# Attention inside a fused MoE kernel: scores of a step in one tile of two PSUM banks, one exponential of 768 columns, and a bank shared by maxima and small products

## The chip, the cores and the metric

The kernel runs on one core of a Trainium2 chip. The metric is the device time of one execution in microseconds (us). Before the change three runs gave 666.51, 666.72 and 667.41 us, median 666.72 us.

## The reference

Three stages follow each other: an attention whose mask compares hash buckets of queries and keys, a mixture of experts with one expert per token, and a two-layer block with a clipped gate. The change is in the attention alone (2 batches, 8 heads each, 768 positions, 64 dimensions per head).

```python
def _attn_ref(q, k, v, proj):
    scale = 1.0 / np.sqrt(D)
    q_bits = np.einsum('bhsd,dk->bhsk', q, proj) > 0
    k_bits = np.einsum('bhsd,dk->bhsk', k, proj) > 0
    mask = q_bucket[:, :, :, None] == k_bucket[:, :, None, :]
    scores = np.where(mask, scale * np.matmul(q, k.T), -1e9)
    attn = np.exp(scores - np.max(scores, axis=-1, keepdims=True))
    attn = attn / (np.sum(attn, axis=-1, keepdims=True) + 1e-09)
    return np.matmul(attn, v)

x = _attn_ref(q, k, v, proj)        # then tokens x 512
x = _moe_ref(x, w_gate, w1, w2, capacity)
return _moe2_ref(x, w_in, w_out)    # h * clip(h + 3, 0, 6) / 6 between two products
```

## The kernel before

The schedule is written out by hand: each engine runs its instructions in the order in which the program issues them, and an engine waits where an operand or a buffer isn't free. The attention is a loop of 96 steps (16 heads with 6 blocks of 128 keys, `STEPS = NC * NH`, L753 and L826 to L847), with a tail of six more turns. One turn `k` issues, in this order:

1. what is due at `k - 0.5` (helpers that were booked for a time in steps with `at` and `spread`, L771 to L782);
2. on ScalarE `high(k - 1)`: a copy of the exponentials in 16 bits (`phi`);
3. `scores(k)` (L437): for each half of 384 queries two matmuls into one PSUM tile `pst` (L445, L446), and one exponential on ScalarE from there into half of the SBUF tile `pf` (L447);
4. `low(k - 2)`: the rest `plo = pf - phi`, on GpSimd, or on VectorE;
5. `mx(k + 8)` (L422): the row maxima, eight steps ahead: for each half one matmul into a tile `psm` (L428) and one VectorE reduction from it (L431);
6. in odd turns `pv(k - 5)` and `pv(k - 4)` (L463): 18 small matmuls each, which add a head's sums over the values (`psv`);
7. what is due at `k`.

Helpers book further work into the same queues: `bits(g)` (L392) makes the hash bits of four heads, two tiles `psb` that VectorE reads at L390; `vgate(r)` (L528) multiplies values of two heads by the gate's weights, tile `psg`, read by VectorE at L546 and L547 for one head and, a step later, for the other; `vscale(g)` (L564) takes the largest value of four heads through a transpose `psn` and a product `pso`; `route` (L208) and `any_unmatched` (L608) use one tile each. `vsplit(h)` (L678) prepares the values of a head on ScalarE and VectorE (L686). `evac(h)` (L495) divides a finished head's sums on VectorE (L483, L486, L491); it is booked by `Q["ev"]` half a step after the turn that issues the head's last sums (L804).

PSUM has eight banks of 512 columns of 32 bits. They stand in four pools, and a tile of a pool takes the next of its buffers in turn; the first instruction that writes it waits until the last reader of the tile that was there is done:

```python
        ps_t = opened(actx, "ps_t", 2, space=PSUM)
        ps_m = opened(actx, "ps_m", 3, space=PSUM)
        ps_v = opened(actx, "ps_v", 2, space=PSUM)
        ps_x = opened(actx, "ps_x", 1, space=PSUM)
```

So scores have two banks, maxima three, the sums over values two, and all the small products of the helpers (`misc`, L346) one. At the start of the kernel the tiles of `ps_v` also hold the first bits (`psb0`, L727), and `ps_t` and `ps_v` hold idle matmuls (`heat`, L321) that keep TensorE busy.

Of the kernel before, what the change touches and what calls it, by code (L numbers as in the profile page):

```python
# [19 lines left out]
P = 128  # L20
# [43 lines left out]
def moe_attention_kernel(ctx, tc, qk, v, vt, pj, wg, w1, w2, win, wout, out, cap):  # L64
# [142 lines left out]

    def route(b, psum):  # L208

# [26 lines left out]
        yield  # L236
        dve.tensor_tensor(out=sc, in0=k3, in1=o, op=ALU.mult)
        yield
        dve.tensor_reduce(out=pos[:, b], in_=sc, axis=AX.X, op=ALU.add)
# [61 lines left out]

    Q = {'v': (-3.25, -4.75, -1.75, -2.25), 'vg': (-4.5, -4.75), 'vgd': 1, 'pr': (-13.0, -12.75, -12.0, -12.5), 'prd': 0.6, 'b0': 7.75, 'b': 1.75, 'bd': 0.5, 'vm0': (8.0, 8.25, 10.75, 13.0), 'vm': (-0.5, 4.75, 7.0, 12.25), 'vs': 13.25, 'pa': 1.5, 'ev': 0.5, 'lvt': -5.0, 'v4': (2.0, 3.75, 4.0, 16.25), 'vg0': (1.85, -4.4, 7.75), 'p2': 3.5, 'lr': (0, 3, 1.5, 4.5), 'lv': 5.5, 'vsd': 0.75, 'ac': (0, 0, 2, 6, 7, 8, 9, 10), 'hd': (3, 5, 17), 'hn': (1, 3, 2, 0, 2, 0, 0, 0), 'ap': (0,), 'h0': (7,), 'hl': (4, 7, 10), 'l0': (), 'll': (1,), 'ht': (6, 3, 7, 6, 3, 2)}

# [3 lines left out]
    with ExitStack() as actx:  # L307
# [4 lines left out]
        ps_t = opened(actx, "ps_t", 2, space=PSUM)  # L312
        ps_m = opened(actx, "ps_m", 3, space=PSUM)
        ps_v = opened(actx, "ps_v", 2, space=PSUM)
        ps_x = opened(actx, "ps_x", 1, space=PSUM)

        idle_sb = pa.tile([P, 512], F16, tag="idle", name="idle_sb")
# [3 lines left out]
        def heat(pool_, tag, n, cols=512):  # L321

            if pool_ not in heat_t:
                heat_t[pool_] = pool_.tile([P, 512], F32, tag=tag, name=f"heat{tag}")
            for _ in range(n):
                pe.matmul(heat_t[pool_][:, :cols], idle_sb[:, 0:P], idle_sb[:, :cols], start=True, stop=True)
# [17 lines left out]
        vr_t, vt_t, vh_t, am_t, sc_t, sw_t = {}, {}, {}, {}, {}, {}  # L344

        def misc(name):  # L346
            return ps_x.tile([P, 512], F32, tag="x", name=name)

# [43 lines left out]
        def bits(g, tiles=None):  # L392
# [20 lines left out]
            for n in range(2):  # L413
                if not tiles:
                    for i in range(4):
                        dot(n, i)
                    yield
                rows(n)
                if not tiles:
                    yield  # L420

        def mx(n):  # L422
# [3 lines left out]
            for n in range(2):  # L426
                ps = ps_m.tile([P, 512], F32, tag="m", name=f"psm{h}{c}{n}")
                pe.matmul(  # L428
# [8 lines left out]
        def scores(k):  # L437
            h, j = divmod(k, NC)
            st = sets[h % 4]
            pf = pf_t[k] = pt.tile([P, S], F32, tag="pf", name=f"pf{k}", bufs=4)  # L440
            kc = slice(j * P, (j + 1) * P)
            for n in range(2):
                ps = ps_t.tile([P, 512], F32, tag="t", name=f"pst{k}{n}")
                qc = slice(n * HS, (n + 1) * HS)
                pe.matmul(ps[:, :HS], st["K1"][:, kc], st["Y"][:, qc], start=True, stop=False)  # L445
                pe.matmul(ps[:, :HS], st["K2"][0:77, kc], st["X"][0:77, qc], start=False, stop=True)  # L446
                act.activation(  # L447
                    pf.rearrange("k (c n p) -> k c n p", c=NC, n=2)[:, :, n],
                    ps[:, :HS].rearrange("k (p c) -> k c p", c=NC), AF.Exp, scale=0.125 / SC / SC,
                )  # L450

# [11 lines left out]
        def pv(k):  # L463
            h, j = divmod(k, NC)
            if j == 0:
                pv_t[h] = ps_v.tile([P, 512], F32, tag="v", name=f"psv{h}")
            hi, lo = phi_t.pop(k), plo_t.pop(k)
# [60 lines left out]
        def vgate(r):  # L528
# [13 lines left out]
            for hh in range(2):  # L542
# [6 lines left out]
                    op0=ALU.mult, op1=ALU.subtract,  # L549
                )  # L550
                yield

# [11 lines left out]
        def vscale(g, fresh=misc):  # L564
# [14 lines left out]
            am2 = ph.tile([n, 1], F32, tag=f"am2{n}", name=f"am2{g}")  # L579
            dve.tensor_reduce(out=am2, in_=ps[0:n, 0:P], axis=AX.X, op=ALU.max)  # L580
            if n > 1:
                a, am2 = am2, ph.tile([n, n], F32, tag="dg", name="dg")
# [6 lines left out]
            a = ph.tile([P, n], F32, tag=f"am3{n}", name=f"am3{g}")  # L589
            dve.tensor_copy(a, ps[:, 0:n])  # L590
            a = a.bitcast(I32)
            x = ph.tile([P, 2 * n - 1], I32, tag=f"ex{n}", name=f"ex{g}")
# [116 lines left out]
        act.activation(st["K2"][0:D], r0[D:P], AF.Copy, scale=SC)  # L709
        pre = [prep(h, h == 0) for h in range(3)]  # L710
        for n in range(2):
            for i, t in enumerate(("X", "K2")):
                c = slice(n * HS, (n + 1) * HS)
                ps = (ps_m, ps_t)[i].tile([P, 512], F32, tag="mt"[i], name=f"psf{n}{i}")
                pe.matmul(
# [10 lines left out]
        DOT = (5,)  # L726
        b0 = bits(0, [ps_v.tile([P, 512], F32, tag="v", name=f"psb0{n}") for n in range(2)])  # L727
        for n in range(NC):
# [72 lines left out]
        for h in range(NH):  # L801
# [6 lines left out]
            elif h < NH - 1:  # L808
                at(k + Q["pa"], pair, h // 2)
                at(NC * h + Q["lvt"], load_vt, h // 2 + 1)  # L810
        spread(66, route(0, lambda: misc("psr0")), 1.5)
        spread(84, weigh(0))
# [699 lines left out]
```

## Time and profile before

| what | value |
|---|---|
| median of three runs | 666.72 us |
| the profiled execution's own time | 666.91 us |
| its span, first to last instruction | 665.2 us |
| TensorE matmul busy | 635.3 us (96%) |
| VectorE busy | 478.9 us (72%) |
| ScalarE busy | 425.3 us (64%) |
| GpSimd busy | 226.5 us (34%) |
| maxima, L431 on VectorE, x192 | 96.3 us, 548 ns each |
| exponentials, L447 on ScalarE, x192 | 83.4 us, 486 ns each |
| attention, first to last sum over values | 36.2 to 233.9 us |

The times come from one execution that the hardware profiler recorded. A line of the trace has the start, the length, the engine, the source line, the operation and its tiles; in brackets stands how long the engine had been idle before it, and which engine, tile and line ended that. PE is TensorE's matmul, PEld its loading of weights, DVE VectorE, ACT ScalarE, POOL GpSimd. Matmuls overlap, so that the distance from start to start says more than the lengths do.

### The profile page before, as it was taken

The page shows a single profiled execution, that of the slowest core. Times are in us where ns is not written, and L with a number is a line of the kernel's source. Part 1 is how long each engine was busy: PE and PEld are TensorE (multiplying, and loading weights), DVE is VectorE, ACT ScalarE, POOL GpSimd, SP SyncE. Part 2 cuts the span into 40 slices and gives each one's busy share as a digit, 9 for nine tenths or more (in the row PEclk, how much of TensorE's full clock was granted, in tenths as well). Part 3 has the DMA queues.
Part 4 walks back from the last instruction along what each step waited for, and adds up shares of the span by engine and source line. Part 5 has one row for each costly group of instructions (what it writes and reads, how often), then busy time and mean ns, then how long its engine had stood idle before and what let it go on. Part 6 is the DMA issues. An engine that isn't in the chain of part 4 may idle for free.

```text
span 665.2 us, 14405 instructions
## 1 busy us (share of the span) xinstructions
PE 635.3 (96%) x5534; PEld 479.4 (72%) x5534; DVE 478.9 (72%) x1041; ACT 425.3 (64%) x867; POOL 226.5 (34%) x198
## 2 busy tenths in 40 slices
PE   6899999999999879999999999999999999999893
PEld 2689888889898749999999996555555555555541
DVE  6778888898999888888888887888888342222320
ACT  2668878778787747777667765544555586555830
POOL 5357869769778133121366500000000021000011
PEclk8989999999999899999999999999999999999998
DMA  8685764774464339877677733444441010000011
GB/s 240 144 227 136 239 171 125 219 182 119 102 175 154 101 100 316 265 242 241 216 255 252 235 117 99 154 148 138 152 134 64 1 63 33 1 0 1 1 49 52
DMA packets 38642, 94.14 MB, mean 142 GB/s; under 512 B 9146, under 2 KB 14522, under 8 KB 38562
## 3 DMA queue, kind: packets, MB, share of 16 engines
q1 hardware_dynamic: 35474, 85.71, 43.1%
q0 software_dynamic: 2400, 7.36, 3.2%
q8 instruction: 46, 0.75, 0.5%
q14 instruction: 34, 0.28, 0.1%
q10 hardware_dynamic: 688, 0.03, 0.1%
HBM read 67.14 MB, written 6.29 MB: 110 GB/s over the span
## 4 chain that ended last, share of the span: by engine, by line
PE 55%; ACT 3%; DMA 2%; DVE 2%; issue 1%; POOL 0%; POOLq 0%; DVEq 0%
PE psg L1287 16%; PE pso L1314 15%; PE psy L1065 11%; PE psh L1038 11%; DMA out_dram<-os,inv 2%; ACT junk L1241 1%; PE psa L1015 1%; ACT gh L1297 1%; DVE rl L1290 1%; ACT rl L1289 0%; PE heat L1117 0%; DVE wl L164 0%; POOL out_dram L1329 0%; PE psw L296 0%; DVE os L1321 0%
## 5 line engine op out<-in xcount | busy, mean ns | idle before, releaser
L461 POOL TENSOR_TENSOR plo<-pf,phi 128x768 f16<-128x768 f32 x85 | 145.0, 1732 | 45.1 <-ACT phi L455 21.4
L447 ACT ACTIVATE pf<-pst 128x384 f32<-128x384 f32 x192 | 83.4, 486 | 44.5 <-PE pst L446 41.2
L431 DVE TENSOR_REDUCE mx<-psm 128x1 f32<-128x384 f32 x192 | 96.3, 548 | 21.5 <-PE psm L428 21.3
L1329 POOL DMA_INDIRECT out_dram<-os,inv x12 | 12.2, 1014 | 270.6 <-DVE os L1321 244.3
L164 DVE SCALAR_TENSOR_TENSOR wl<-raw,wh 128x1024 f16<-128x1024 f32 (+1 forms) x68 | 83.2, 1227 | 5.9 <-ACT wh L158 5.2
L1287 PE MATMUL psg<-yTh,ch 128*128 128x512 f16 (+1 forms) x256 | 83.4, 326 | 3.2 <-DVE rl L1290 3.2
L1287 PE MATMUL psg<-yTl,ch 128*128 128x512 f16 (+1 forms) x256 | 83.4, 326 | 0.0
L1287 PE MATMUL psg<-yTh,cl 128*128 128x512 f16 (+1 forms) x256 | 83.4, 326 | 0.0
L1290 DVE SCALAR_TENSOR_TENSOR rl<-rl,psg 128x512 f32<-128x512 f32 x64 | 35.0, 550 | 64.5 <-ACT rl L1289 64.0
L445 PE MATMUL pst<-Y,K 128*128 128x384 f32 x192 | 75.4, 393 | 1.8 <-ACT pf L447 1.7
L1287 PEld LDWEIGHTS <-ch 128*128 128x128 f16 x512 | 50.1, 98 | 35.9
L1314 PE MATMUL pso<-ch,gh 128*128 128x512 f16 x192 | 72.8, 379 | 0.0
L1314 PE MATMUL pso<-ch,gl 128*128 128x512 f16 x192 | 72.8, 379 | 0.0
L1314 PE MATMUL pso<-cl,gh 128*128 128x512 f16 x192 | 72.8, 379 | 0.0
L455 ACT ACTIVATE phi<-pf 128x768 f16<-128x768 f32 x83 | 70.0, 844 | 1.9
L428 PE MATMUL psm<-K,X 76*128 76x384 f32 x192 | 65.8, 421 | 4.7 <-DMA X<-b 2.1
L1314 PEld LDWEIGHTS <-gh 128*128 128x128 f16 x384 | 37.6, 98 | 42.3
L158 ACT ACTIVATE wh<-raw 128x1024 f16<-128x1024 f32 (+1 forms) x68 | 67.6, 998 | 0.5 <-issue 0.5
L1065 PE MATMUL psy<-hh,wl 128*128 128x224 f16 x256 | 66.3, 259 | 0.0
L1065 PE MATMUL psy<-hh,wh 128*128 128x224 f16 x256 | 66.3, 259 | 0.0
L1065 PE MATMUL psy<-hl,wh 128*128 128x224 f16 x256 | 66.3, 259 | 0.0
L446 PE MATMUL pst<-X,K 77*128 77x384 f32 x192 | 66.1, 344 | 0.0
(231 smaller groups left out, 1494.6 us busy)
## 6 DMA issues: line engine op xcount, KB each, us to landing
raw<-in_w_dram SPq DMA_DIRECT2D x64, 512.0 KB
rc<-in_win_dram SPq DMA_DIRECT2D x16, 512.0 KB
rc<-in_wout_dram SPq DMA_DIRECT2D x16, 512.0 KB
r<-in_qk_dram SPq DMA_DIRECT2D x16, 384.0 KB
K<-hi SPq DMA_DIRECT2D x31, 192.0 KB
vr<-in_v_dram SPq DMA_DIRECT2D x4, 768.0 KB
vt<-in_vt_dram SPq DMA_DIRECT2D x8, 384.0 KB
Y<-hi SPq DMA_DIRECT2D x16, 192.0 KB
```

The lines of the kernel that those rows point to most:

```text
L158: act.activation(wh[e, i][:, c : c + n], r, AF.Copy, scale=(S1, S2)[i // 2])
L164: dve.scalar_tensor_tensor(out=wl[e, i][:, c : c + n], in0=r, scalar=(S1, S2)[i // 2], in1=wh[e, i][:, c : c + n], op0=ALU.mult, op1=ALU.s ...
L431: dve.tensor_reduce(out=mm[:, c, n : n + 1], in_=ps[:, :HS], axis=AX.X, op=ALU.max)
L445: pe.matmul(ps[:, :HS], st["K1"][:, kc], st["Y"][:, qc], start=True, stop=False)
L446: pe.matmul(ps[:, :HS], st["K2"][0:77, kc], st["X"][0:77, qc], start=False, stop=True)
L447: act.activation(pf.rearrange("k (c n p) -> k c n p", c=NC, n=2)[:, :, n], ps[:, :HS].rearrange("k (p c) -> k c p", c=NC), AF.Exp, scale=0 ...
L455: act.activation(phi_t[k], pf_t[k], AF.Copy)
L461: eng.tensor_tensor(out=plo_t[k], in0=pf_t.pop(k), in1=phi_t[k], op=ALU.subtract)
L1038: pe.matmul(ps, l[:, c], r[:, k], start=n == 0, stop=n == 3 * KD - 1)
L1065: pe.matmul(ps, l, r, start=n == 0, stop=n == 3 * KF - 1)
L1287: pe.matmul(ps, l, x, start=n == 0, stop=n == 3 * KD - 1)
L1314: pe.matmul(po[blk][s], l, r, start=first and n == 0, stop=last and n == 2)
```

## The change

- `ps_t` keeps two buffers, but a buffer is now a tile of two banks (`pair_of`). `scores(k)` writes both halves into one such tile with its four matmuls, and one exponential of 768 columns follows in place of two of 384.
- `ps_m` has two buffers in place of three, and `ps_v` one in place of two. Every third tile of the maxima is taken from `ps_x`, the bank of the small products, unless a small product is in use by the program's order (`in_use`, set by `misc` and cleared by `misc_read` where the last reader has been issued).
- `evac` is booked at the turn itself (`Q["ev"]` is 0.0 in place of 0.5), so that VectorE gets it ahead of what is due half a step later.
- At the start the first bits (`psb`) and the first products for head 0 (`psf`) use the paired tiles.

```diff
-        ps_m = opened(actx, "ps_m", 3, space=PSUM)
-        ps_v = opened(actx, "ps_v", 2, space=PSUM)
+        ps_m = opened(actx, "ps_m", 2, space=PSUM)
+        ps_v = opened(actx, "ps_v", 1, space=PSUM)
         ps_x = opened(actx, "ps_x", 1, space=PSUM)
+
+        def one_of(pool_, tag, name):
+            return pool_.tile([P, 512], F32, tag=tag, name=name)
+
+        def pair_of(name):
+            return ps_t.tile([P, 2, 512], F32, tag="t", name=name)
...
+        in_use = [False]
+        nmx = [0]
+
         def misc(name):
-            return ps_x.tile([P, 512], F32, tag="x", name=name)
+            in_use[0] = True
+            return one_of(ps_x, "x", name)
+
+        def misc_read():
+            in_use[0] = False
+
+        def for_mx(name):
+            nmx[0] += 1
+            if nmx[0] % 3 or in_use[0]:
+                return one_of(ps_m, "m", name)
+            return one_of(ps_x, "x", name)
...
                 rows(n)
                 if not tiles:
+                    misc_read()
                     yield
...
-                ps = ps_m.tile([P, 512], F32, tag="m", name=f"psm{h}{c}{n}")
+                ps = for_mx(f"psm{h}{c}{n}")
...
+            ps = pair_of(f"pst{k}")
             for n in range(2):
-                ps = ps_t.tile([P, 512], F32, tag="t", name=f"pst{k}{n}")
                 qc = slice(n * HS, (n + 1) * HS)
-                pe.matmul(ps[:, :HS], st["K1"][:, kc], st["Y"][:, qc], start=True, stop=False)
-                pe.matmul(ps[:, :HS], st["K2"][0:77, kc], st["X"][0:77, qc], start=False, stop=True)
-                act.activation(
-                    pf.rearrange("k (c n p) -> k c n p", c=NC, n=2)[:, :, n],
-                    ps[:, :HS].rearrange("k (p c) -> k c p", c=NC), AF.Exp, scale=0.125 / SC / SC,
-                )
+                pe.matmul(ps[:, n, :HS], st["K1"][:, kc], st["Y"][:, qc], start=True, stop=False)
+                pe.matmul(ps[:, n, :HS], st["K2"][0:77, kc], st["X"][0:77, qc], start=False, stop=True)
+            act.activation(
+                pf.rearrange("k (c n p) -> k n c p", c=NC, n=2),
+                ps[:, :, :HS].rearrange("k n (p c) -> k n c p", c=NC), AF.Exp, scale=0.125 / SC / SC,
+            )
...
-                pv_t[h] = ps_v.tile([P, 512], F32, tag="v", name=f"psv{h}")
+                pv_t[h] = one_of(ps_v, "v", f"psv{h}")
...
                     op0=ALU.mult, op1=ALU.subtract,
                 )
+                if hh:
+                    misc_read()
                 yield
...
-        b0 = bits(0, [ps_v.tile([P, 512], F32, tag="v", name=f"psb0{n}") for n in range(2)])
+        psb = pair_of("psb")
+        b0 = bits(0, [psb[:, n] for n in range(2)])
```

`misc_read()` is also called behind the reads of `psn` and `pso` in `vscale`, and, through a new argument, behind the read in `route` at L237; `any_unmatched` has no such call.

## Rows read from the trace of the kernel before

**Rows 1.** Busy time by stretch: PE, PEld, DVE, ACT, POOL (x instructions), granted clock, DMA share, GB/s.
```profile
40.00:205.00 165.00, 162.13 (x1969) 145.88 (x1968) 144.53 (x328) 129.60 (x241) 129.71 (x85) 1.00 0.60 161
205.00:235.00 30.00, 27.68 (x395) 23.75 (x395) 26.83 (x67) 23.99 (x47) 9.77 (x8) 0.94 0.38 123
```

**Rows 2.** Waits from 40 to 205 us: who waited for whom, total us, times, longest.
```profile
DVE mx L431 <- PE psm L428: 14.3, 21, 1.3
...
PE psm L428 <- DVE mx L431: 1.9, 6, 0.4
...
PE pst L445 <- ACT pf L447: 0.8, 3, 0.3
```

**Rows 3.** ScalarE by line and shape, 0 to 250 us: busy, mean ns | idle before.
```profile
L447 ACT ACTIVATE pf<-pst 128x384 f32<-128x384 f32 x192 | 83.4, 486 | 44.5 <-PE pst L446 41.2 <-DVE phi L457 1.9 <-POOL lg L510 0.4
L455 ACT ACTIVATE phi<-pf 128x768 f16<-128x768 f32 x83 | 70.0, 844 | 1.9
```

**Rows 4.** Timeline of turns 34 to 37.
```profile
101.02 0.88 ACT L447 ACTIVATE pf<-pst 128x384 f32<-128x384 f32 x2 [1.72 <-PE pst L446]
...
105.14 0.39 PE L428 MATMUL psm<-K,X 76*128 76x384 f32 x1
105.79 0.44 PE L445 MATMUL pst<-Y,K 128*128 128x384 f32 x1 [0.26 <-ACT pf L447]
105.93 0.27 DVE L547 SCALAR_TENSOR_TENSOR vh<-psg,sw,vh 128x48 f16<-128x48 f32 x1
```

**Rows 5.** Timeline of turns 24 and 25.
```profile
78.40 0.39 PE L428 MATMUL psm<-K,X 76*128 76x384 f32 x1
78.62 0.49 PE L428 MATMUL psm<-K,X 76*128 76x384 f32 x1
79.63 0.27 DVE L547 SCALAR_TENSOR_TENSOR vh<-psg,sw,vh 128x48 f16<-128x48 f32 x1
79.68 0.39 PE L428 MATMUL psm<-K,X 76*128 76x384 f32 x1
80.41 0.55 PE L428 MATMUL psm<-K,X 76*128 76x384 f32 x1 [0.34 <-DVE mx L431]
```

**Rows 6.** Timeline of turns 26 and 27.
```profile
83.26 0.56 DVE L431 TENSOR_REDUCE mx<-psm 128x1 f32<-128x384 f32 x1
83.38 0.85 PE L401 MATMUL psb<-r,pj_sb 128*32 128x384 f32 x8
85.08 0.60 DVE L390 TENSOR_SCALAR b<-psb,pj_sb 128x384 fp32r<-128x384 f32 x1
85.20 0.39 PE L428 MATMUL psm<-K,X 76*128 76x384 f32 x1
```

**Rows 7.** Timeline of the first turns.
```profile
19.35 0.44 PE L445 MATMUL pst<-Y,K 128*128 128x384 f32 x1
20.04 0.61 DVE L390 TENSOR_SCALAR b<-psb,pj_sb 128x384 fp32r<-128x384 f32 x1
33.69 0.53 PE L428 MATMUL psm<-K,X 76*128 76x384 f32 x1 [2.07 <-DMA X<-b]
```

**Rows 8.** Busy time by stretch, near that last wait.
```profile
32.00:33.00 1.00, 0.00 (x0) 0.00 (x0) 0.00 (x0) 1.00 (x3) 0.00 (x0) 1.00 1.05 353
35.00:36.00 1.00, 1.00 (x5) 0.87 (x3) 0.28 (x1) 0.71 (x2) 0.26 (x1) 0.50 0.96 347
```

**Rows 9.** Timeline of the attention's last turns.
```profile
205.08 0.56 DVE L431 TENSOR_REDUCE mx<-psm 128x1 f32<-128x384 f32 x1 [0.50 <-PE psm L428]
216.41 0.61 DVE L491 TENSOR_TENSOR xp<-psv,rd 128x432 f32<-128x432 f32 x1
217.35 0.21 PE L473 MATMUL psv<-vh,phi 128*128 128x73 f16 x1
229.43 0.45 PE L445 MATMUL pst<-Y,K 128*128 128x384 f32 x1 [0.62 <-ACT pf L447]
```

More of the change, by code (lines that the diff above doesn't have):

```diff
@@ L206, in spots, with route @@
         )
-    def route(b, psum):
+    def route(b, psum, read=lambda: None):
         n = NC
@@ L237, in route @@
         dve.tensor_tensor(out=sc, in0=k3, in1=o, op=ALU.mult)
+        read()
         yield
@@ L299, in windows @@
                 )
-    Q = {'v': (-3.25, -4.75, -1.75, -2.25), 'vg': (-4.5, -4.75), 'vgd': 1, 'pr': (-13.0, -12.75, -12.0, -12.5), 'prd': 0.6, 'b0': 7.75, 'b': 1.75, 'bd': 0.5, 'vm0': (8.0, 8.25, 10.75, 13.0), 'vm': (-0.5, 4.75, 7.0, 12.25), 'vs': 13.25, 'pa': 1.5, 'ev': 0.5, 'lvt': -5.0, 'v4': (2.0, 3.75, 4.0, 16.25), 'vg0': (1.85, -4.4, 7.75), 'p2': 3.5, 'lr': (0, 3, 1.5, 4.5), 'lv': 5.5, 'vsd': 0.75, 'ac': (0, 0, 2, 6, 7, 8, 9, 10), 'hd': (3, 5, 17), 'hn': (1, 3, 2, 0, 2, 0, 0, 0), 'ap': (0,), 'h0': (7,), 'hl': (4, 7, 10), 'l0': (), 'll': (1,), 'ht': (6, 3, 7, 6, 3, 2)}
+    Q = {'v': (-3.25, -4.75, -1.75, -2.25), 'vg': (-4.5, -4.75), 'vgd': 1, 'pr': (-13.0, -12.75, -12.0, -12.5), 'prd': 0.6, 'b0': 7.75, 'b': 1.75, 'bd': 0.5, 'vm0': (8.0, 8.25, 10.75, 13.0), 'vm': (-0.5, 4.75, 7.0, 12.25), 'vs': 13.25, 'pa': 1.5, 'ev': 0.0, 'lvt': -5.0, 'v4': (2.0, 3.75, 4.0, 16.25), 'vg0': (1.85, -4.4, 7.75), 'p2': 3.5, 'lr': (0, 3, 1.5, 4.5), 'lv': 5.5, 'vsd': 0.75, 'ac': (0, 0, 2, 6, 7, 8, 9, 10), 'hd': (3, 5, 17), 'hn': (1, 3, 2, 0, 2, 0, 0, 0), 'ap': (0,), 'h0': (7,), 'hl': (4, 7, 10), 'l0': (), 'll': (1,), 'ht': (6, 3, 7, 6, 3, 2)}
     HT = Q["ht"]
@@ L323, in heat @@
             if pool_ not in heat_t:
-                heat_t[pool_] = pool_.tile([P, 512], F32, tag=tag, name=f"heat{tag}")
+                heat_t[pool_] = pair_of(f"heat{tag}")[:, 0] if pool_ is ps_t else one_of(pool_, tag, f"heat{tag}")
             for _ in range(n):
@@ L580, in vscale @@
             dve.tensor_reduce(out=am2, in_=ps[0:n, 0:P], axis=AX.X, op=ALU.max)
+            misc_read()
             if n > 1:
@@ L590, in vscale @@
             dve.tensor_copy(a, ps[:, 0:n])
+            misc_read()
             a = a.bitcast(I32)
@@ L710, in moe_attention_kernel @@
         pre = [prep(h, h == 0) for h in range(3)]
+        psf = pair_of("psf")
         for n in range(2):
@@ L713, in moe_attention_kernel @@
                 c = slice(n * HS, (n + 1) * HS)
-                ps = (ps_m, ps_t)[i].tile([P, 512], F32, tag="mt"[i], name=f"psf{n}{i}")
+                ps = psf[:, n] if i else one_of(ps_m, "m", f"psf{n}{i}")
                 pe.matmul(
@@ L810, in moe_attention_kernel @@
                 at(NC * h + Q["lvt"], load_vt, h // 2 + 1)
-        spread(66, route(0, lambda: misc("psr0")), 1.5)
+        spread(66, route(0, lambda: misc("psr0"), misc_read), 1.5)
         spread(84, weigh(0))
```

## The prediction

> **What bounds the kernel now.** I read the busy time by stretch first, then the waits of the attention, then the timeline around each place where a helper uses the shared bank. From 40 to 205 us TensorE is busy for 162.1 of 165 us at full clock, ScalarE for 129.6 and VectorE for 144.5 [rows 1]. The waits say which of them paces: VectorE waited 21 times for the matmul of a maximum, 14.3 us in all, while TensorE waited only six times for a maximum's reduction and three times for an exponential with a bracket of its own [rows 2]. So up to 205 us TensorE sets the pace, with VectorE close behind; VectorE's work comes in runs that begin where a matmul lets it go on. A new wait of TensorE is then time lost, unless VectorE was about to stop it anyway; a faster ScalarE is worth only the three waits on it. From 205 us on it is the other way round: VectorE is busy for 26.8 of 30 us [rows 1], and its last wait of some length for a maximum is the 0.50 us at 205.08 [rows 9].
>
> **The exponential.** 96 instructions go. One of 384 columns takes 486 ns [rows 3], but two behind each other take 0.88 us [rows 4], since they overlap. One of 768 has not been run; the copy of 768 columns takes 844 ns [rows 3]. Below it is bounded by the 486 ns of half its columns, above by twice that, 972 ns; I take 0.82 us, nearest to the copy, as PSUM is its only difference in the reading. That saves 0.06 us of 0.88 per step, 96 x 0.06 = 6 us of ScalarE. It lies beside TensorE and is worth nothing there: ScalarE had 35 us idle from 40 to 205 [rows 1]. The Trainium skill (Perfetto Trace Analysis, Optimizing Scalar/DVE Operations) says that grouping helps where the engine is saturated, and that where it isn't but stalls others, breaking work up lets some finish sooner. By that the merged exponential is a step backwards: it starts only after four matmuls instead of two. The trace doesn't let this count, as the next paragraph says.
>
> What is later: the exponential ends up to 0.35 us later, since its second half no longer overlaps the first half's end, and `phi`, `plo` follow. Their user `pv` comes four to five turns, over 8 us, later, so nothing waits in the middle. What is gained is that TensorE may run two turns ahead of the exponential in place of one: the three waits of 0.26 us at turns like that of 105.79 [rows 4] go. I count them below where they belong.
>
> **One bank for the sums of values.** The first `pv` of the next head must now wait for the whole `evac`. Its end stood ahead of that matmul for all 15 heads, mostly by 0.9 to 2.6 us; the nearest is 216.41 + 0.61 = 217.02 against 217.35 [rows 9], 0.33 us. `evac` also moves forward on VectorE. Cost 0; were the move to give nothing and VectorE 1 us later, one such place would cost 0.7 us. What `evac` passes on VectorE's queue are readers of the bits and gate products due within half a step; its 1.1 us delays them by as much as it was delayed before.
>
> **The shared bank, the large term.** By the program's order I wrote down which tile follows which in each bank, before and after, and set beside it when VectorE finished the old reader and when TensorE came to the new writer. For the old banks this gives the places where the trace shows TensorE waiting for a maximum's reduction, and no other. For the new ones it gives two kinds of wait:
>
> *A maximum behind a gate product.* `vgate` releases the bank in the program where its last read is issued, and the same turn's second maximum (or the next third tile) takes it. VectorE gets to that read late. In turn 24 the read ends at 79.63 + 0.27 = 79.90 and TensorE came at 78.62 [rows 5]: 1.28 us. A turn later TensorE had to wait for VectorE anyway: 79.68 to 80.41 is 0.73 against 0.22 for an undisturbed pair (78.40 to 78.62), so 0.51 of it is absorbed and 0.77 stays. Turn 48 repeats it. In turn 36 the read ends at 105.93 + 0.27 = 106.20 and TensorE came at 105.14 [rows 4]: 1.06, of which the 0.26 wait for the exponential is absorbed, 0.80 stays; turn 60 repeats it. Turn 72: 0.52 by the same reckoning, less the third 0.26: 0.26. Turn 84 lies behind 205 us, where VectorE paces: 0. The gate product of turns 10 to 12 has no maximum behind it in time: 0. Sum 2 x 0.77 + 2 x 0.80 + 0.26 = 3.4 us.
>
> *A small product behind a maximum.* `bits` issues its matmuls directly behind a turn's maxima, and the bank's last user is the first of them. In turn 26 its reduction ends at 83.26 + 0.56 = 83.82, TensorE came at 83.38 [rows 6]: 0.44. The maximum after it must wait until 85.08 + 0.60 = 85.68 and came at 85.20; having lost 0.44 it waits 0.04 more. Sum 0.48. Seven places have this form (three of `bits`, three transposes of `vscale`, one of `route`): 3.4 us. Behind the products of `vscale` there are three more of 0.2 to 0.3 us, each one turn ahead of a wait for VectorE as in turn 25, which takes it in: 0. Where a helper holds the bank, the maxima go on with two; by the same list that alone costs at most 0.1 us in two turns.
>
> Together +6.8 us. Bounds: +2.5, if VectorE's runs begin earlier than the rows show and half the waits are taken in, to +9 with nothing taken in.
>
> **The start.** `scores(0)` now writes the paired tile that held the first bits, whose second read ends at 20.04 + 0.61 = 20.65; it started at 19.35 [rows 7]: 1.30 us later. Farther on TensorE stood for 2.07 us until a DMA of bits had landed at 33.69 [rows 7]; these DMAs hang on the same reads by VectorE and not on the scores, so the wait shrinks to 0.77. After the 2.07 us the granted clock fell to 0.50 [rows 8], the lower of its two levels (1.2 GHz), for about 3.3 us, which cost half of that, 1.6 us. Waits like the 0.34 us at 80.41 left it at 1.00 [rows 5, 1]. The 0.77 is nearer to those: I take -1.6 us. Bounds: -1.6, and +1.3 if the new wait at 19.35 makes the clock fall or isn't covered.
>
> **The end of the attention.** Behind 205 us VectorE's list is unchanged. In the last turns TensorE and ScalarE wait for each other: 0.62 at 229.43 [rows 9] and that goes with two turns of room, while the last exponential ends up to 0.35 later. I take -0.3, between -1.0 and +0.4. Later stages don't change.
>
> **Sum.** 666.91 (own time of the profiled execution; its span is 665.2) + 6.8 - 1.6 - 0.3 = 671.8. The median of the runs is 0.2 below the profiled one: 671.6 us, 0.7% slower.
>
> **The rivals.**
> *A, faster: VectorE's clock takes the new waits in.* Mechanism: a wait on the shared bank ends with VectorE, so if VectorE's run there sets the next stop of TensorE anyway, it costs nothing, and only the gains stay: 3 x 0.26, 1.6 and up to 1.0, so 666.7 - 3.4 = 663.3. For it: VectorE is busy 144.5 of 165 us, and three small waits are taken in so already. Against: it waited 21 times for TensorE [rows 2], which means that its runs start late when TensorE is late. It decides from two thirds of the 6.8 us taken in. The Trainium skill (Perfetto Trace Analysis, Matmul Optimizations) asks that all eight banks be in use for parallel work; by it a bank that only small products used is better shared. The rows say that all eight have users before, and that the shared one is asked for at its worst moment.
> *B, no change:* half of the waits taken in, gains in full: 666.7 + 3.4 - 1.6 - 1.0 = 667.5.
> *C, slower still: the clock falls in the middle.* Four waits of 1.1 to 1.5 us lie between the 0.3 us that left the clock alone and the 2.07 us that didn't [rows 5, 7, 8]. At 1.6 us each: 671.6 + 6.4 = 678.0.
>
> **Chances.** Forecast 0.62 (own range 668.3 to 674.5), A 0.15, B 0.11, C 0.12. A difference of 0.2%, 1.3 us, is about what can be told from none here. Faster 0.15, same 0.10, slower 0.75. The range from 666.5 to 677.0 leaves out A and the upper end of C.
>
> **What would show it.** Right: at turns 24, 36, 48 and 60 the second maximum waits for a reader of `psg` by 1.0 to 1.5 us; the first matmul of `psb` and `psn` for a reduction by 0.4; no wait on `pf` before 205 us; 96 exponentials of about 0.82 us; `scores(0)` behind the bits, and the wait at 33.69 below 1 us. Wrong: waits there that leave the later turns on their old times, a wait of the sums on `evac`, or a clock below 1.00 between 40 and 205 us.

## The result: 677.6 us, 1.4% slower

The changed kernel's median is 677.61 us (675.14 to 680.18, 6 runs) against 667.35 us (666.51 to 671.94) for the kernel before: ratio 1.0143, 95% interval 1.0113 to 1.0172. The forecast was 671.6 with a range to 677.0: the direction was right, the size was not. The profiled execution took 677.13 us with a span of 675.4; with that of before (666.91) the difference is 10.2 us, and the attention alone accounts for 9.9.

**The profile after.** The busy time by stretch answers to [rows 1]; two short stretches of it follow, in which the granted clock was near or at 0.50, the lower of its two levels (1.2 GHz). The waits of TensorE from 40 to 205 us answer to [rows 2].

```profile
40.00:205.00 165.00, 156.54 (x1858) 141.09 (x1857) 137.59 (x311) 120.11 (x157) 119.56 (x81) 0.99 0.58 156
205.00:235.00 30.00, 27.25 (x336) 25.23 (x333) 27.39 (x70) 22.06 (x30) 16.79 (x12) 0.95 0.53 162
170.00:174.00 4.00, 4.00 (x44) 3.80 (x43) 1.70 (x6) 1.65 (x2) 1.53 (x1) 0.59 0.47 140
35.00:40.00 5.00, 5.00 (x46) 4.70 (x45) 2.93 (x8) 2.27 (x3) 2.51 (x2) 0.50 1.03 258
```

```profile
PE psm L449 <- DVE vh L568: 3.6, 5, 0.9
PE psn L600 <- DVE mx L452: 1.6, 3, 0.7
PE psb L421 <- DVE mx L452: 1.3, 3, 0.4
PE psm L449 <- DVE mx L452: 0.8, 2, 0.5
PE psr L232 <- DVE mx L452: 0.5, 1, 0.5
PE psm L449 <- DVE sc L237: 0.4, 1, 0.4
```

TensorE is busy for 5.6 us less of the same 165 us. The waits on an exponential are gone, as forecast; in their place stand maxima (`psm`) behind the readers of gate products (`vh`) and small products (`psn`, `psb`, `psr`) behind reductions, the two kinds that were forecast.

ScalarE by line, 0 to 250 us (busy, mean ns | idle before), answers to [rows 3]. One exponential of 768 columns takes 804 ns, 0.82 was taken.

```profile
L468 ACT ACTIVATE pf<-pst 128x768 f32<-128x768 f32 x96 | 77.1, 804 | 60.0 <-PE pst L467 57.4 <-DVE nflag L643 2.0 <-POOL plo L482 0.7
```

The timeline at the places of [rows 4 to 6]: start, duration, operation, and in brackets the wait with what ended it.

```profile
81.64 0.55 PE L449 MATMUL psm<-K,X 76*128 76x384 f32 x1
82.72 0.27 DVE L568 SCALAR_TENSOR_TENSOR vh<-psg,sw,vh 128x48 f16<-128x48 f32 x1
83.05 0.56 PE L449 MATMUL psm<-K,X 76*128 76x384 f32 x1 [0.85 <-DVE vh L568]
...
87.08 1.02 DVE L452 TENSOR_REDUCE mx<-psm 128x1 f32<-128x384 f32 x2 [0.40 <-PE psm L449]
87.69 0.85 PE L421 MATMUL psb<-r,pj_sb 128*32 128x384 f32 x8 [0.43 <-DVE mx L452]
...
109.83 0.27 DVE L568 SCALAR_TENSOR_TENSOR vh<-psg,sw,vh 128x48 f16<-128x48 f32 x1
110.16 0.55 PE L449 MATMUL psm<-K,X 76*128 76x384 f32 x1 [0.82 <-DVE vh L568]
```

In turn 24 the second maximum could come right behind the first at 81.64, but its bank is read by VectorE until 82.72 + 0.27 = 82.99. From start to start the delay is 83.05 - 81.64 - 0.22 = 1.19 us, in the reckoning that forecast 1.0 to 1.5; the bracket, 0.85, counts only the idle time behind the first matmul's end. In turn 26 the bits wait 0.43 us, where 0.44 was worked out.

The start, against [rows 7], then turn 63 and the end, against [rows 9]:

```profile
6.12 0.60 DVE L410 TENSOR_SCALAR K<-psf,pj_sb 12x384 fp32r<-12x384 f32 x1
6.78 0.11 PEld L741 LDWEIGHTS psf<-r,pj_sb 64*12 64x12 f32 x2 [1.30 <-DVE K L410]
8.27 0.61 DVE L410 TENSOR_SCALAR K<-psf,pj_sb 12x384 fp32r<-12x384 f32 x1 [0.80 <-PE psf L741]
...
20.10 0.45 PE L466 MATMUL pst<-Y,K 128*128 128x384 f32 x1
20.25 1.14 DVE L410 TENSOR_SCALAR b<-psb,pj_sb 128x384 fp32r<-128x384 f32 x2
34.08 0.99 PE L449 MATMUL psm<-K,X 76*128 76x384 f32 x2 [1.69 <-DMA X<-b]
...
168.69 0.55 PE L449 MATMUL psm<-K,X 76*128 76x384 f32 x1 [0.50 <-DVE mx L452]
169.69 0.27 PE L600 MATMUL psn<-ident,am 128*1 128x128 f32 x1 [0.44 <-DVE mx L452]
...
213.55 0.61 DVE L512 TENSOR_TENSOR xp<-psv,rd 128x432 f32<-128x432 f32 x1
216.92 0.21 PE L494 MATMUL psv<-vh,phi 128*128 128x73 f16 x1
220.06 0.55 PE L449 MATMUL psm<-K,X 76*128 76x384 f32 x1 [0.72 <-DVE vh L568]
```

Two lines of before belong beside it: the last read of `psf`, and the granted clock from 35 to 40 us.

```profile
7.57 0.60 DVE L390 TENSOR_SCALAR K<-psf,pj_sb 12x384 fp32r<-12x384 f32 x1
```

```profile
35.00:40.00 5.00, 5.00 (x50) 4.53 (x49) 3.06 (x9) 3.61 (x7) 2.10 (x2) 0.73 1.02 297
```

The first scores start before VectorE begins to read the first bits, so they did not wait for them: they got the other pair tile, that of the idle matmuls. So a pool does not always give out its buffers in turn; why it did not here is not shown. What makes turn 0 late by 0.75 us stands at 6.78: the two halves of the first products for head 0 (`psf`) are now one pair tile, and the weight load for the second half waits until VectorE has read the first half, at 6.12 + 0.60 = 6.72. Before, they were two tiles and nothing waited; the last read began at 7.57 in place of 8.27.

The wait for the DMA is 1.69 us instead of 0.77, and the clock fell behind it, for longer than before: from 35 to 40 us it was 0.50 against 0.73. One bank for the sums costs nothing: the evacuation ends at 214.16, the next product comes at 216.92, and no matmul of this trace waits for an evacuation.

**Where the 10 us went.** The table gives how far the first matmul of scores of a turn starts behind the same turn of before. The forecast's terms are sorted by the turns at which they were placed; the second and third trace of the changed kernel come from the last experiments.

| turns | forecast | first trace | second | third |
|---|---|---|---|---|
| to 7 | -1.6 | +1.7 | +1.0 | +2.5 |
| 7 to 15 | +1.0 | +1.4 | +1.9 | +3.5 |
| 15 to 62 | +4.6 | +3.3 | +5.6 | +8.4 |
| 62 to 66 | +0.5 | +2.9 | +2.9 | +1.6 |
| 66 to 88 | +0.7 | +1.9 | +2.0 | +1.7 |
| 88 to 95 | -0.3 | -1.4 | -1.3 | -2.9 |
| sum | +4.9 | +9.9 | +12.0 | +14.9 |
| own time | 671.8 | 677.13 | 680.02 | 684.03 |

### The profile page after: what moved, and what is told of

Its sections match the earlier page's. It is cut to its first block, busy times and chain, and to the rows that moved or that the text cites. A ratio compares the mean times of both kernels' runs of the same rounds, so it can differ in the third digit from the quotient of the medians.

```text
span 675.4 us, 14317 instructions
## 1 busy us (share of the span) xinstructions
PE 640.2 (95%) x5534; PEld 484.8 (72%) x5534; DVE 480.3 (71%) x1041; ACT 419.7 (62%) x771; POOL 223.4 (33%) x198
## 4 chain that ended last, share of the span: by engine, by line
PE 55%; ACT 3%; DMA 2%; DVE 2%; issue 1%; POOL 0%; POOLq 0%; DVEq 0%
PE psg L1314 16%; PE pso L1341 15%; PE psy L1092 11%; PE psh L1065 11%; DMA out_dram<-os,inv 2%; ACT junk L1268 1%; PE psa L1042 1%; ACT gh L1324 1%; DVE rl L1317 1%; ACT rl L1316 0%; PE heat L1144 0%; DVE wl L164 0%; POOL out_dram L1356 0%; PE psw L297 0%; DVE os L1348 0%
## 5 line engine op out<-in xcount | busy, mean ns | idle before, releaser
L482 POOL TENSOR_TENSOR plo<-pf,phi 128x768 f16<-128x768 f32 x85 | 142.6, 1701 | 57.2 <-ACT phi L476 24.7
L468 ACT ACTIVATE pf<-pst 128x768 f32<-128x768 f32 x96 | 77.1, 804 | 60.0 <-PE pst L467 57.4
L1356 POOL DMA_INDIRECT out_dram<-os,inv x12 | 11.8, 987 | 270.9 <-DVE os L1348 244.3
L449 PE MATMUL psm<-K,X 76*128 76x384 f32 x192 | 71.5, 443 | 7.5 <-DVE vh L568 4.3
L466 PE MATMUL pst<-Y,K 128*128 128x384 f32 x192 | 72.3, 377 | 0.0
L449 PEld LDWEIGHTS psm<-K,X 76*128 76x128 f32 x192 | 54.0, 311 | 18.4 <-DVE mx L452 6.2
L494 PE MATMUL psv<-vh,phi 128*128 128x73 f16 x576 | 66.6, 201 | 0.0
```

Of the source, the lines that this page charges most:

```text
L449: pe.matmul(ps[:, :HS], st["X"][0:76, c::NC], st["K2"][0:76, n * HS : (n + 1) * HS], start=True, stop=True)
L466: pe.matmul(ps[:, n, :HS], st["K1"][:, kc], st["Y"][:, qc], start=True, stop=False)
L468: act.activation(pf.rearrange("k (c n p) -> k n c p", c=NC, n=2), ps[:, :, :HS].rearrange("k n (p c) -> k n c p", c=NC), AF.Exp, scale=0.1 ...
L482: eng.tensor_tensor(out=plo_t[k], in0=pf_t.pop(k), in1=phi_t[k], op=ALU.subtract)
```

## The experiments

Medians of before on the chip of each group: 669.1 (first four), 666.9 (next eight), 667.5 (last three). Executions of one kernel spread over up to 10 us, the longer ones mostly at a lower mean granted clock (of the kernel "shared apart", 0.995 at 668.3 us and 0.981 at 678.0), so that the turn-by-turn differences of a trace say more than its total.

**Which part costs? Sharing, the exponential, or the third bank.** Four kernels take the change apart. The first keeps all of it but the sharing; the second keeps all but the single exponential; the third is the kernel before with the sharing alone (two banks of maxima and the spare one, single score tiles); the fourth keeps the maxima off the shared bank in 28 turns near small products.

```
first:   - if nmx[0] % 3 or in_use[0]: ps_m else ps_x      + always ps_m
second:  - act.activation(768 columns)                     + for n in range(2): act.activation(ps[:, n, :HS])
third:   before, with ps_m 3 -> 2, for_mx() and misc_read() of the change
fourth:  - if nmx[0] % 3 or in_use[0]:   + if nmx[0] % 3 or in_use[0] or turn[0] in NEAR:
```

> The changed kernel, but the maxima never take the small products' bank: they have two banks always. Theory (waits on the shared bank, and the falls of the clock that follow them, make the whole loss): no wait on a reader of psg or by psb and psn on a maximum; two banks bring waits of up to 0.7 us where VectorE's runs are long, mostly where the kernel before waited too; 667 to 672 us, 5 to 10 below the changed kernel. Rival 1 (the pair tile and the later exponential make the loss): 676 to 678, as the changed kernel. Rival 2 (the loss of the third bank for maxima makes it): 678 to 685, since it is now gone altogether.

> The changed kernel, but with two exponentials of 384 columns out of the pair tile. Theory (shared bank): as the changed kernel within 1.5 us, 676 to 679, since ScalarE isn't waited for. Rival 1 (the merged exponential): back by most of the loss, 667 to 671.

> The kernel before, with one part of the change alone: two banks for the maxima and every third of their tiles from the small products' bank. Theory (shared bank): 672 to 677, the same waits of 1.0 to 1.3 us on psg as in the changed kernel. Rival 1 (exponential): 666 to 668.

> The changed kernel, but in the turns beside a small product (28 of 96) the maxima don't take its bank. Theory (shared bank): no wait of 1 us on psg and none of psb or psn on a maximum; 666 to 671, at or below the run without sharing. Rival 2 (too few banks for maxima): no better than the changed kernel, 677 to 680.

Unshared: 678.69 us, ratio 1.0155 (1.0112 to 1.0197), in the range of rival 2. The theory that only the shared bank costs falls: without it the maxima have two banks, and wait for their own reductions instead. In the profiled execution (674.93, the fastest of four, with a granted clock of 1.00 there) from 40 to 205 us:

```profile
PE psm L447 <- DVE mx L450: 2.8, 6, 0.9
```

```profile
PEld psm L447 <- DVE mx L450: 10.1, 37, 1.3
```

(The second is the weight load of the same matmuls, which waits first; the changed kernel has 3.8 us in 14 such waits.)

Split exponential: 675.38, 1.0101 (1.0060 to 1.0142), just under the range of the theory and far above the rival's: the single exponential is not the cause of the loss, and the interval overlaps that of the changed kernel, so it is not shown to be worth or to cost anything. The Trainium skill (Perfetto Trace Analysis, Optimizing Scalar/DVE Operations) says that breaking up instructions may let work finish sooner where they hold up other engines. In the changed kernel no matmul waits for an exponential from 40 to 205 us.

Sharing alone: 681.52, 1.0176 (1.0131 to 1.0221), above the theory's range: two own banks and the shared one bring the whole loss without pair tile or single exponential. Its turn 0 is only 0.14 us late.

Shared apart: 672.86, 1.0058 (1.0027 to 1.0090), between the two ranges: from turn 15 to 62 only +1.0, but +6.2 by turn 15. The exempt turns 7 to 18 had two banks, and a clock fall stands at 56 us; the kernel "apart, late" below shares in these turns and has +1.8.

**What is a bank for maxima worth?** Two, four and a pair, on the kernel before.

```
two:     - ps_m = opened(actx, "ps_m", 3, space=PSUM)    + 2
four:    + ps_m 4, ps_v 1, 'ev': 0.0, first bits in one ps_t and one ps_v tile
merged:  + ps_m 2 tiles [P, 2, 512], one tensor_reduce over axis XY of 768; ps_v 1, 'ev': 0.0, first bits as in four;
         half of the first products for head 0 (psf) in one such tile
```

> The kernel before with two banks for the maxima products in place of three, and nothing else changed: single score tiles, two exponentials of 384, two banks for sums of values, the eighth bank for small products alone. Theory (the third maxima bank is what costs: with two, the first product of a turn waits for a reduction of the turn before whenever VectorE is late, as the 39 waits of 10.7 us in all show where the changed kernel had its maxima in two banks): 675 to 681 us, and the waits on L431 by the products of L428 come to 8 to 12 us between 40 and 212 us. Rival (two banks were short only because the pair tile and the single exponential moved the scores against the maxima): 667 to 670 us, with under 3 us of such waits.

> The kernel before with the second bank for sums of values given to the maxima products (four banks instead of three), the last evacuation half a turn earlier, and the first random bits in one bank of the scores and one of the sums; scores and exponentials as before. Theory (before, TensorE is busy 162.1 of 165 us in the middle, so a fourth bank finds little to take away, and one bank for the sums costs nothing, as no wait for it shows in the changed kernel): 664 to 668 us, same as before. Rival 1 (each further bank for the maxima is worth some us, as the third is): 658 to 663 us. Rival 2 (the one bank for sums is what costs): 671 to 677 us with waits of the products of values on the evacuation.

> Kernel before with the eight banks split another way: two single banks for scores and two exponentials of 384 as before, but the maxima of a turn in one tile of two banks, two such tiles, with one reduction of 768 columns in place of two of 384; one bank for sums of values, one for small products, nothing shared. Theory (TensorE bounds the middle and only its waits can be lost or won; with four banks for maxima few are left, and the merged reduction shortens VectorE's line, 96 instructions fewer of 0.55 us against a longer one under 1.1 us): 662 to 667 us. Rival (a pair tile is freed only by the whole reduction, so that two tiles wait as two banks do): 672 to 680 us, with 5 to 12 us of waits of the maxima products on their reduction.

Two banks: 676.67, 1.0119 (1.0067 to 1.0171), with the waits of the theory (6.0 us of weight loads and 2.0 of matmuls from 40 to 205). So losing the third bank alone costs in all about what the whole change costs, 9.8 us against 10.3, and the sharing as written gives nothing back in the total. But the places differ. The kernel of two banks is 2.4 us late at turn 0 and 4.8 at turn 15, and loses 4.8 more from turn 15 to 88; sharing alone, which differs from it by the sharing, is 0.14 and 2.2 late there, and loses 14.7 in its trace, with two clock falls. So the shared bank helps with the first maxima and costs more than it gives behind them, and that the totals are alike is partly chance.

Four: 668.83, 1.0021 (0.9994 to 1.0048), no difference, a little above the theory's range. Turns 15 to 62 win 2.4 us, as every wait on a reduction goes, but the end gives it back:

```profile
215.69 0.19 PE L473 MATMUL psv<-vh,phi 128*128 128x73 f16 x1 [0.85 <-DVE xp L491]
...
219.96 0.20 PE L614 MATMUL psu<-un,ones 128*1 128x8 f32 x2 [2.10 <-DVE un L611]
```

TensorE comes sooner to an end that VectorE paces: the flag product waited 1.41 us before and waits 2.10 now, and there the single bank of sums does cost 0.85. Merged: 673.58, 1.0090 (1.0059 to 1.0122): turns 15 to 62 win 2.3, the start loses 4.6, with clock falls at 41 and 55 us, and the end 2.0. The number lies in the rival's range, but the rival's waits are not there: from 40 to 205 us no product of a maximum waits for a reduction.

**The clock falls.** The changed kernel with eight idle matmuls more in turn 4 and no sharing in turns 61 to 64; and the kernel before with scores that start late, as the forecast had it.

```
no falls:   - 'hn': (1, 3, 2, 0, 2, ...)  + 'hn': (1, 3, 2, 0, 10, ...);   + or turn[0] in (61, 62, 63, 64)
late start: + heat(ps_t, "t", 6) ahead of turn 0, kernel before
```

> The changed kernel with eight more idle matmuls in turn 4, ahead of the maxima product that waited there for the DMA of the row of maxima (34.1 us), and with the maxima kept out of the shared bank in turns 61 to 64, where two waits close together came before the granted clock of 0.50. Theory (the fall after the start and the fall at turn 63 are each a term of their own, about 1.7 and 2.4 us): 672.5 to 674.5 us, the turn-by-turn difference to before shrinks at turn 7 to 10 and at turns 62 to 65, and the granted clock stays at 1.00 through 34 to 42 us. Rival 1 (the falls hide in waits that are there anyway, and the third bank missing in turns 61 to 64 takes back what it gives): 676 to 679 us. Rival 2 (the added matmuls, 8 of 0.21 us, lie on the path and cost as much as the fall does): gain at turn 62 only, 674.5 to 676 us.

> The kernel before with six more idle matmuls ahead of turn 0, so that the first scores start 1.3 us later, which is what the prediction had expected of the change. Theory of the prediction (the wait for the row of maxima at 33.7 us shrinks by what the start is late, the clock doesn't fall behind it, and 1.6 us are won): turn 6 starts 1 us or more earlier, 664.5 to 666.5 us. Rival (what is won at turn 6 is given back by turn 10, where the next loads haven't landed, as with the eight idle matmuls in turn 4 of the changed kernel): turn 10 within 0.5 us of before, 666.5 to 668.5 us.

No falls: 677.85, 1.0157 (1.0099 to 1.0215), rival 1. At turn 7 it is 0.7 us ahead of before, at turn 15 2.0 behind again: the sooner products wait 1.01 us at 43.26 for loads of `vr`. The fall at turn 63 is gone (62 to 66: +1.5), but one stands behind the wait of turn 49:

```profile
35.00:40.00 5.00, 5.00 (x59) 4.65 (x59) 3.97 (x10) 3.79 (x5) 3.17 (x2) 1.00 1.03 272
140.00:142.00 2.00, 2.00 (x27) 2.00 (x26) 1.28 (x2) 1.10 (x2) 1.23 (x2) 0.50 0.91 244
```

Late start: 668.41, 1.0011 (0.9991 to 1.0031), no difference. The mechanism of the forecast's start is right and its worth nil: the DMA wait shrinks from 2.07 to 0.91, the clock stays at 1.00 from 33 to 41 us (0.79 before), turn 7 is 1.35 us ahead, and turn 11 0.2. What was won is lost where VectorE waits for the next transfer (second line), and TensorE for VectorE behind it, 0.60 us at 42.33.

```profile
33.77 0.75 PE L428 MATMUL psm<-K,X 76*128 76x384 f32 x2 [0.91 <-DMA X<-b]
...
40.23 1.58 DVE L378 SCALAR_TENSOR_TENSOR lo<-r,hi 128x768 fp32r<-128x768 f32 x1 [1.21 <-DMA Y<-lo]
```

**Sharing without the bad moments, and a mend of the end.**

```
apart, late:   the fourth kernel's list NEAR without its turns below 24, and with 63
held longer:   misc_read():  + until[0] = nmx[0] + 5;    for_mx(): + or nmx[0] <= until[0]
later flag:    two yields more ahead of misc("psu"), on before; four, later flag: the same on four banks
```

> The changed kernel with the maxima kept out of the shared bank in the 23 turns from 24 on that lie next to small products (turns 24 to 27, 36 to 38, 48 to 51, 60 to 63 and others); the first 23 turns share as the change does. Theory (what costs after the start is the waits of maxima for the readers of small products and the clock fall behind them, while two banks alone in those few turns cost less): the start as in the changed kernel, 3 us behind at turn 15, and from there to turn 88 at most 3 us more in place of 8: 671 to 674 us. Rival (two banks in those turns cost as much as the waits, as in the kernel with two banks all through, or a clock fall comes somewhere else): 675 to 679 us.

> The changed kernel with the shared bank kept from the maxima for five more products after each last reader of a small product (some two turns), so that no product of maxima stands right behind such a reader; small products still come behind maxima as before. Theory (the waits of maxima on the readers, 0.8 us each at turns 24, 36, 48 and 60 and 0.5 to 0.7 at 72 and 84, are one half of the loss behind the start, and the small products that wait for a reduction, 0.4 us each, the other): from turn 15 to 88 about 4 us in place of 8, no waits on the readers of the gates' products: 672 to 675 us. Rival 1 (two banks in those turns cost what the readers cost): 676 to 679 us. Rival 2 (the readers are all of it): under 2.5 us from turn 15 to 88, 669 to 671.5 us.

> The kernel before with the small product on the unmatched rows (L614, which waited 1.41 us for VectorE at 220.9 us, with the granted clock at 0.5 behind it) put one and a half turns later. Theory (that wait and the clock fall behind it are worth 1 to 3 us): 664 to 666 us. Rival (the tail is paced by VectorE, and the wait moves to another product): 666.5 to 668 us.

> The kernel with four banks for maxima and one for sums, and besides the small product on the unmatched rows put one and a half turns later. Theory (the middle wins 2 to 3 us by the fourth bank, and the tail, which took it back, is mended by the later product): 662 to 665 us. Rival (the tail is bound by VectorE, whatever the order, and takes back what the middle wins): 666 to 669 us.

Apart, late: 673.22, 1.0090 (1.0055 to 1.0125), the theory: +1.8 at turn 15, and from there to turn 88 +2.3 where the three traces of the change have 8.1 to 11.8. Two banks in a few turns are cheap, two banks all through are not (4.8 and 5.0 in those turns, in the kernels "two" and "unshared").

Held longer: the median 675.56, 1.0133 (1.0099 to 1.0166), just misses the theory's range, the profiled execution (671.52) makes it: no wait on a gate's reader, no clock fall, +3.1 from turn 15 to 88, of which 1.2 to turn 62. What is left there is small products behind maxima and two banks (`psm` <- `mx`), and the other executions, at a mean clock of 0.983 to 0.986 in place of 0.994, were 4 to 7 us longer.

```profile
PE psm L451 <- DVE mx L454: 2.8, 6, 1.0
PE psr L232 <- DVE mx L454: 1.1, 1, 1.1
PE psb L423 <- DVE mx L454: 0.4, 1, 0.4
```

Later flag: 668.13, 1.0018 (0.9999 to 1.0037); the wait of 1.41 goes and turns 88 to 95 win 2.5 us in its trace, but a clock fall at 50 us, where before had none, took 1.4, and over 12 runs nothing is won. This fall stands behind no wait of a matmul that the trace shows from 42.5 us on, so a fall can come without one. Four banks with it: 669.58, 1.0035 (1.0014 to 1.0057), above both ranges. No version beat the kernel before.

**Is it the same in every execution?** The changed kernel twice more.

> The changed kernel once more, unchanged, for a second trace. If the clock fall near 171 us belongs to the two waits ahead of it at turn 63, it is there again, and turns 62 to 66 lose 2.5 to 3 us again; if it comes by chance, it is gone or elsewhere, and turns 62 to 66 lose 0.5 to 1.5 us.

> The changed kernel a third time, unchanged. As for the second trace: the start 1.5 to 3.5 us behind before at turn 15 in every trace if the loss there is the change's; turns 8 to 62 lose 4 to 6 us in every trace, if those waits are the change's; the place of a clock fall tells whether it is tied to turn 63.

680.02 and 684.03 us. The loss is there each time; the clock falls are not in the same places: the one at turn 63 is there again in the second trace and missing in the third. The third trace leaves the expected ranges: it is 6.0 us behind at turn 15, with the clock at 0.50 twice, from 36 and from 43 us on. From turn 8 to 62 the three traces lose 4.8, 7.6 and 11.1 us, where 4 to 6 was expected.

The second trace, a wait from its timeline and the stretches with falls:

```profile
82.84 0.56 PE L449 MATMUL psm<-K,X 76*128 76x384 f32 x1 [0.85 <-DVE vh L568]
```

```profile
84.00:88.00 4.00, 4.00 (x44) 3.90 (x44) 2.26 (x3) 2.09 (x4) 3.26 (x2) 0.57 0.81 207
172.00:178.00 6.00, 6.00 (x54) 5.70 (x54) 3.60 (x10) 2.73 (x4) 3.05 (x3) 0.72 0.39 110
```

The same trace at turn 39, where the clock stayed at 1.00:

```profile
115.92 0.55 PE L449 MATMUL psm<-K,X 76*128 76x384 f32 x1 [0.49 <-DVE mx L452]
116.92 0.27 PE L600 MATMUL psn<-ident,am 128*1 128x128 f32 x1 [0.44 <-DVE mx L452]
```

```profile
113.00:121.00 8.00, 6.95 (x93) 6.08 (x92) 6.82 (x15) 5.29 (x7) 4.98 (x5) 1.00 0.60 151
```

The third trace, the waits at turns 39, 49 and 63, and the stretches behind them; the last stayed at full clock:

```profile
119.06 0.55 PE L449 MATMUL psm<-K,X 76*128 76x384 f32 x1 [0.49 <-DVE mx L452]
120.05 0.27 PE L600 MATMUL psn<-ident,am 128*1 128x128 f32 x1 [0.44 <-DVE mx L452]
...
143.70 0.56 PE L449 MATMUL psm<-K,X 76*128 76x384 f32 x1 [0.85 <-DVE vh L568]
...
176.78 0.55 PE L449 MATMUL psm<-K,X 76*128 76x384 f32 x1 [0.50 <-DVE mx L452]
177.77 0.27 PE L600 MATMUL psn<-ident,am 128*1 128x128 f32 x1 [0.44 <-DVE mx L452]
```

```profile
120.00:124.00 4.00, 3.95 (x45) 3.86 (x46) 2.05 (x6) 1.77 (x3) 1.88 (x2) 0.70 0.61 161
144.00:148.00 4.00, 4.00 (x45) 3.90 (x45) 2.74 (x5) 2.76 (x4) 2.80 (x3) 0.68 0.67 165
177.00:183.00 6.00, 5.43 (x57) 4.82 (x58) 4.52 (x13) 4.15 (x6) 3.30 (x4) 1.00 0.54 140
```

From turn 15 to 88 the clock falls behind turns 25, 39, 49 or 63, always behind a wait that the change made (the third trace has one more fall, at 87 us, behind turn 25). None of these waits brings a fall each time: 0.85 us at turn 25 left it at 1.00 in the first trace, 0.49 and 0.44 at turn 39 in the second, 0.50 and 0.44 at turn 63 in the third. One fall is priced by the same turns of the traces with and without it: turns 63 to 66 1.5 against 0.2, turns 25 to 28 1.3 against -0.2, turns 49 to 52 1.3 against -0.2, turns 38 to 44 2.5 against 1.1. So 1.3 to 1.5 us each; from turn 15 to 88 there was one, two and three of them in the three traces, and none in the kernel before's.

The kept traces of all kernels, seventeen, bear this out. From 60 to 205 us the granted clock is 0.96 to 0.99 in the six of kernels whose maxima share the bank next to small products (the three traces of the change, "split exponential", "sharing alone" and "no falls"), and 1.00 in the eleven others, among them "apart, late" and "held longer", which share it only at other moments. What decides whether a single wait is followed by a fall is open. The changed kernel's first trace, then "apart, late":

```profile
60.00:205.00 145.00, 136.96 (x1634) 124.01 (x1634) 122.25 (x279) 107.06 (x141) 106.74 (x73) 0.99 0.57 157
```

```profile
60.00:205.00 145.00, 142.19 (x1703) 128.62 (x1702) 125.68 (x286) 110.54 (x147) 112.52 (x76) 1.00 0.61 164
```

## Why the prediction was right in kind and wrong in size

Against the own time of 671.8 that was summed, 677.13 was measured: 5.3 us more, term by term.

- **The start failed** (-1.6 forecast, +1.7 measured to turn 7: 3.3 us). The step "`scores(0)` now writes the paired tile that held the first bits" is wrong for this program: it got the other pair and started before the bits were read. So the wait for the DMA stayed, and the clock fall with it. And the late-start kernel shows that the step was worth nothing even if it had held, as the next transfers are waited for. What is late instead is VectorE's list: the first bits are read at 20.25, when the second read was already under way at 20.04 before. The forecast had no term for the cause, the pair tile of `psf`, whose second half waits for the reading of the first. Two comparisons show its price: turn 0 is 0.75 late in the changed kernel and 0.14 in "sharing alone", which has the same banks for maxima and single tiles for `psf`; and it is 3.2 late in "unshared" and 2.4 in the kernel of two banks, which again lacks the pair tiles. So it is 0.6 to 0.8 us. The merged kernel, which has such a pair too, shows the same wait and is 1.7 late. The eight traces with the change's start have 0.75 to 1.5; what makes the rest in some of them is open. From turn 5 to 7 the first trace loses 1.1 more, where the clock stays at 0.50 for longer.
- **The waits in the middle held.** Places and kinds are as listed. The gate waits measure 0.85, 0.82, 0.85, 0.83 by their brackets and 1.19, 0.99, 1.19, 1.01 from start to start; turn 26 is 0.7 us later than turn 24 by the first of them, where 0.77 was to be left. The bits wait 0.43 in place of 0.44. Less their clock falls, turns 15 to 62 cost 3.3, 4.1 and 4.1 in the three traces (4.6 forecast), and turns 7 to 84 of the first 7.5 (6.8). "The maxima go on with two; that alone costs at most 0.1 us" was too low by about 1 us, as held longer (+1.2 from turn 15 to 62) and apart, late (+0.9) show.
- **The clock was the rival's, not nil.** Rival C had it fall behind the new waits, with a chance of 0.12 and at 1.6 us a fall. It does, one to three times from turn 15 to 88 of a trace, at 1.3 to 1.5 us. The argument against was that 0.34 us at 80.41 left the clock alone [rows 5]; that says nothing of 0.85 us, nor of 0.50 and 0.44 within one turn, which the first trace has at turn 63 (62 to 66: +2.9 in place of 0.5, 1.3 of it the fall). Rival C's 678.0 came nearer than the forecast by luck: it counted four falls behind the gate waits, 6.4 us, where this trace has one, 1.3, at another wait, and it kept the start's -1.6.
- **"Turn 84 lies behind 205 us, where VectorE paces: 0"** failed: the wait at 220.06 is 0.72, and turn 85 is 1.0 us later. VectorE is behind there, and a bank that it has not released still stops TensorE. But a turn later 0.8 is left of it, and the kernels that keep the shared bank free there (unshared, held longer, apart, late) lose 0.6 by then, so only about 0.2 is the wait's own; the rest comes with two banks. The last turns give some back (-1.4 in place of -0.3), in those kernels too.
- **Held:** the exponential (804 ns, no loss, no gain), one bank for the sums beside this pace of TensorE, no wait on an exponential before 205 us.

Together 3.3 (to turn 7) + 0.4 (7 to 15) - 1.3 (15 to 62) + 2.4 (62 to 66) + 1.2 (66 to 88) - 1.1 (88 to 95) = 4.9 of the 5.3; 0.3 lie behind the attention. The forecast's own upper bounds, +9, +1.3 and +0.4, add up to 677.4; its range ended at 677.0.

So the count of collisions held, and what it left out failed it: the start, and the clock behind the collisions. It also never asked what the third bank is worth. The kernel with two banks shows 9.8 us for it, half of them by turn 15, and a bank that small products hold at the worst moments does not replace it; kept off those moments ("apart, late") the kernel is 0.9% behind before, against 1.2% with two banks, with intervals that overlap.

## What to carry to other kernels

Before a bank is shared, ask who reads it last and how far that engine lags the writer: a bank released behind a lagging engine's queue stops the leading engine until it is read (1.19 us at turn 24). A tile of two banks is waited for as one: here its second half could not be written before its first was read. Price a rotation's depth by taking one buffer away as well as by counting collisions; and price each new wait on the bounding engine with a share of a clock fall on top, since a fall here cost 1.3 to 1.5 us behind waits of under 1 us. A kernel whose executions spread by several us is compared turn by turn, in more than one trace.

## What was not expected of the hardware

- Waits of 0.85 us, or of 0.50 and 0.44 us about 1 us apart, were at times followed by 3 to 4 us at a granted clock of 0.50, at other times by none, in executions of the same program. The Trainium skill (TensorE: Matmul & The Clock Gate, A second HAM failure mode: psum-queue depth-cycling) tells of a kernel whose clock goes up and down because TensorE idles briefly but often as it cycles PSUM banks. These traces agree that the clock falls behind brief idle times at PSUM banks; here single ones were at times enough, and no run prices frequent ones.
- Two exponentials of 384 columns behind each other take 0.87 us, one of 768 0.80: merging saves 0.07, where two single lengths of 486 ns would let one expect 0.17.
- Most of the gains won at one place (1.35 us at the start, 2.4 in the middle, 2.5 at the end) were gone a few turns later or within the spread, handed to a transfer, to VectorE or to a clock fall elsewhere.
